# An attention-plus-GLU kernel: two raw weight buffers, an accumulating store and a reordered front

## The chip, the cores and the metric

The kernel runs on one core of one Trainium2 chip. The metric is the device time of one execution in microseconds (us); the time before is the median of 3 runs, 719.59 us (718.81 to 720.78). One more execution was profiled, and all rows of views are from it. The engines are called PE (TensorE, matrix products), DVE (VectorE), ACT (ScalarE), POOL (GpSimd) and SP (SyncE, which here only issues DMAs). Each engine works through its own instructions in order.

## The reference

The input x has 2048 tokens of width 448. It is layer-normalised without weights, and the output is x plus two branches on the normalised x: an attention with a memory, and a gated feed-forward layer. Cut to what matters:

```python
xn = _layernorm(x)
# attention: 16 heads of 28, 4 segments of 512 tokens
q, k, v = xn @ wq, xn @ wk, xn @ wv
for s in range(4):
    p = softmax(qs @ ks.T * scale + mask)      # mask: keys after the query
    o = g * (phi(qs) @ M) / (phi(qs) @ z + 1e-6) + (1 - g) * (p @ vs)
    M, z = M + phi(ks).T @ vs, z + phi(ks).sum()
# feed-forward: 448 -> 1792 -> 448
h = sigmoid(xn @ w_gate) * (xn @ w_up)
out = x + concat(o) @ wo + h @ w_down
```

## The kernel before, in words

**Precision.** Every operand of a large product is split in two parts: a rounded high part that ACT makes (`split`, L85-87, a copy) and the low rest that DVE makes (a subtraction). A product is then 11 matmuls: high by high, high by low, low by high (`TERMS`, L52). The width of 448 is held in four chunks of 128 rows, whose last holds high and low rows together, so matmuls of the fourth chunk need the low part as well.

**Front (L262-543).** For each of four blocks of 512 tokens: statistics, normalise, transpose on PE and split (`transpose_high`, `transpose_low`, L92-108), values (`value_terms`, L314), keys and queries (`keys_queries`, L330), which are stored in DRAM. For block 0 the order of the first three engines is written out by hand tile by tile (L387-483): `statistics`, `root` (a square root on ACT, L283), `rstd` and `normalise` (L288-309), `split_v` (a part of the value weights: high on ACT, low on POOL). From block 1 on, `recall` (L377) reads the memory: a matmul of `phi` with the state, `weigh` on DVE (L126), and a store of the result to `md` in DRAM from POOL's queue. It has two result buffers `tb` on the chip. The last block's four recalls stand between steps of the feed-forward generator, `FILL` = 3 steps ahead of each (L539-543).

**Feed-forward (`gated`, L158-256).** It is a generator, and PE's program is made by stepping it. The 14 slices of 128 hidden columns are taken in groups of two; a group passes the four blocks. Per block and slice: 22 gate-up matmuls `pgu` (L235), a tanh on ACT, two products on DVE, and later the down matmuls `pd` (L165), whose result DVE adds to `acc` (L168). The weights of a slice arrive as two loads on the SP queue: gate and up into `raw` (L173, one buffer) and down into `rawd` (L177, two buffers). `ready_up` and `ready_down` split them into `wgu` (three buffers, shared with others) and `wdn` (four). The table `ahead` (L212-226) says at which block and slot of a group each load and each split is called. The two halves of the output weights use `raw` as well (`load_out`, L191). One buffer means that a load can't be issued until ACT and DVE have split what is there.

**Attention (L551-708)** is a second generator, spread evenly over the feed-forward's steps by the loop at L750-759. 32 pairs of heads: query and key loads from DRAM (L563, two buffers `qk2`), score matmuls (L579) into two PSUM banks, a copy on ACT (L582), a mask on POOL (L591), maxima on DVE (L594), the shift by the maximum on DVE (L630), exp on ACT (L631). Two pairs make a unit: values by weights (`pa`, L656), a copy (L659), transposes (`n`, L663), `weigh`, and for segments 1 to 3 the memory's part, which is loaded from `md` into a tile `tb` (L648), is added by POOL (L668). The sum is stored to `od` from POOL's queue (L669). `project` (L710) later loads `od` block by block, transposes it, multiplies by wo and adds to `acc` (L742).

PE's order is the order in which the code is run. ACT, DVE, POOL and SP are ordered by a scheduler that the kernel's framework brings, outside the front's hand-written part. Tiles that share a buffer wait for each other by semaphores.

Of the kernel before, what the change touches and what calls it, by code (L numbers as in the profile page):

```python
# [9 lines left out]
F32 = mybir.dt.float32  # L10
F32R = mybir.dt.float32r
AF = mybir.ActivationFunctionType
ALU = mybir.AluOpType
# [3 lines left out]
P = 128  # L17
D = 448
# [36 lines left out]
FRONT = {mybir.EngineType.PE, mybir.EngineType.Activation, mybir.EngineType.DVE}  # L55
FILL = 3
WARM = 10
# [3 lines left out]
def kernel(  # L61
# [23 lines left out]
    def split(hi, lo, src):  # L85
        A.activation(hi, src, AF.Copy)  # L86
        V.tensor_sub(lo, src, hi.bitcast(F32))
# [52 lines left out]
    vd = [dram.tile([P, NT, H * 32], F32, name=f"vd{b}") for b in range(NB)]  # L140
    md = [dram.tile([P, NT, D], F32, name=f"md{b}") for b in range(NB)]
    od = [dram.tile([P, NT, D], F32, name=f"od{b}") for b in range(NB)]
# [15 lines left out]
    def gated():  # L158
# [14 lines left out]
        def load_up(f):  # L173
            raw_up[f] = mid.tile([P, 1024], F32, name="raw", bufs=1)
            nc.sync.dma_start(raw_up[f], w_ffn[f][:, :1024])

        def load_down(f):  # L177
            raw_down[f] = mid.tile([P, D], F32, name="rawd", bufs=2)
            nc.sync.dma_start(raw_down[f], w_ffn[f][:, 1024:])
# [8 lines left out]

        raw_o = {}

        def load_out(h):  # L191
            raw_o[h] = mid.tile([P, 1024], F32, name="raw", bufs=1)[:, :2 * D]
            nc.sync.dma_start(raw_o[h], w_o[:, 2 * D * h:2 * D * (h + 1)])

        def ready_out(h):
            wo[h] = eight_k(F32R, "wo").rearrange("p c n -> p (c n)")
            split(wo[h][:, :2 * D], wo[h][:, 2 * D:4 * D], raw_o[h])

# [5 lines left out]
        load_down(0)  # L204
        load_down(1)
        yield
# [3 lines left out]
        for f0 in range(0, NF, FG):  # L210

            ahead = {}  # L212
            if f0 == 0:
                ahead[0, 0] = lambda: ready_up(1)
            if f0 + FG < NF:
                ahead[0, 2] = lambda: load_up(f0 + 2)
                ahead[1, 2] = lambda: (ready_up(f0 + 2), load_down(f0 + 2))
                ahead[1, 3] = lambda: load_up(f0 + 3)
                ahead[2, 1] = lambda: (ready_down(f0 + 2), load_down(f0 + 3))
                ahead[3, 2] = lambda: ready_up(f0 + 3)  # L220
                ahead[3, 3] = lambda: ready_down(f0 + 3)
            else:

                ahead[0, 2] = lambda: load_out(0)
                ahead[1, 2] = lambda: (ready_out(0), load_out(1))
                ahead[3, 2] = lambda: ready_out(1)
# [35 lines left out]
    with tc.tile_pool(name="front", bufs=2) as sb, tc.manual_schedule(engines=FRONT):  # L262
# [24 lines left out]

        def rstd(mv, vh, y):  # L288

            steps = vh.shape[1]  # L290
            tm = sb.tile([P, steps], F32, name=f"tm{steps}")
            V.reciprocal(y, y)
            if steps == 1:
                V.tensor_scalar(tm, y, y, vh, op0=ALU.mult, op1=ALU.mult)
                V.tensor_scalar(y, tm, 1.5, y, op0=ALU.add, op1=ALU.mult)
            else:
                V.tensor_mul(tm, y, y)
                V.tensor_mul(tm, tm, vh)
                V.scalar_tensor_tensor(y, tm, 1.5, y, op0=ALU.add, op1=ALU.mult)
            return [(mv[:, t, 0:1], y[:, t:t + 1]) for t in range(steps)]  # L300

        def normalise(b, t, mean, y):
            xn = sb.tile([P, 512], F32, name="xn")
            V.tensor_scalar(xn[:, :D], acc[b][:, t, :], mean, y, op0=ALU.subtract, op1=ALU.mult)
            if b == 0:
                A.activation(xn[:, D:], xn[:, 384:D], AF.Copy)
            else:
                G.tensor_copy(xn[:, D:], xn[:, 384:D])
            return xn
# [67 lines left out]
        def recall(b, i, phi):  # L377
            tb = sb.tile([P, NT * HG, DH], F32, name="tb", bufs=2)
            n2 = bank("n2", ("m", "pd")[i % 2] if b < NB - 1 else "m")
            for t in range(NT):  # L380
                T.matmul(n2[:, t * P:(t + 1) * P], phi[:, t * P:(t + 1) * P], mst[b % 2][i], start=True, stop=True)  # L381
            weigh(sb, tb, n2, gate[:, HG * i:HG * (i + 1)], MEM_EPS)
            nc.gpsimd.dma_start(md[b][:, :, GW * i:GW * (i + 1)], tb.rearrange("p (t j) d -> p t (j d)", t=NT))

# [43 lines left out]

        def normalised(t):
            xn[t] = normalise(0, t, *rstd(*st[t], y[t])[0])  # L430

# [3 lines left out]
        normalised(0)  # L435
        split_v(0)
        st[1] = statistics(0, 1, 1)
        y[1] = root(st[1][1])
        split_v(1)
        turn_high(0)  # L440
# [19 lines left out]
        store_values(0, 1, pv[1])  # L460
        normalised(3)
        turn_low(2)
        pv = bank("pv", "p")
        value_terms(0, 2, pv, EARLY[1], 0, 5)
        turn_high(3)
        split_qk(0)
        value_terms(0, 2, pv, EARLY[1], 5)
        store_values(0, 2, pv)
# [11 lines left out]
        for b in range(NB):  # L480
# [57 lines left out]
            if last:  # L538
                phi = [phi_queries(b, i) for i in range(NG)]  # L539
                for i in range(NG):  # L540
                    for _ in range(FILL):
                        next(ffn)
                    recall(b, i, phi[i])
# [7 lines left out]
    class Pair:  # L551
# [53 lines left out]
        def weights(self, mx):  # L605
# [5 lines left out]
            V.tensor_max(m0[:, :, 8:16], m0[:, :, 8:16], mx[:, 64:80].rearrange("p (h n) -> p h n", h=2))  # L611
            up = sb.tile([P, 2, 16], F32, name="up", bufs=2)
            top = sb.tile([P, 2, 16], F32, name="top", bufs=2)
            G.tensor_copy(up[0:64], m0[64:128])
# [19 lines left out]
    class Unit:  # L634
# [9 lines left out]

        def load_memory(self):
            if self.s > 0:
                self.tb = sb.tile([P, NT, GW], F32, name="tb")
                nc.sync.dma_start(self.tb, md[self.s][:, :, GW * self.i:GW * (self.i + 1)])  # L648

        def finish(self):  # L650
# [15 lines left out]
            o3 = on.rearrange("p (t j) d -> p t (j d)", t=NT)  # L666
            if s > 0:
                G.tensor_add(o3, o3, self.tb)  # L668
            nc.gpsimd.dma_start(od[s][:, :, GW * i:GW * (i + 1)], o3)  # L669
            yield  # L670
# [4 lines left out]
    def attention():  # L675
# [5 lines left out]
        for u in range(len(units) + 1):  # L681
            for n in range(2):
                run[n] = pairs[2 * u + n].scores() if u < len(units) else iter(())
            for k, which in enumerate(SLOT):
# [15 lines left out]
                if which == 2 and u > 0:  # L700
                    fin = units[u - 1].finish()
                    next(fin)
                    units[u - 1].load_memory()
                    if u < len(units):
                        units[u].load_values()
# [44 lines left out]
    with tc.manual_schedule(engines=MANUAL):  # L750
        next(steps)
        k = NG * FILL + 6
        for part in (ffn, project()):
            for _ in part:
                want = min(round(n_att * (k - LEAD) / (N_FFN + N_OUT - LEAD - TAIL)), n_att)
                k += 1
                while done < want:
                    next(steps)
                    done += 1
# [38 lines left out]
```

## Time and profile before

| | |
|---|---|
| median of 3 runs | 719.59 us (718.81 to 720.78) |
| the profiled execution's own time | 719.77 us |
| its span in the trace | 718.0 us |
| PE busy | 703.8 us (98%) |
| DVE busy | 557.5 us (78%) |
| ACT busy | 338.2 us (47%) |
| POOL busy | 154.9 us (22%) |
| granted TensorE clock | 1.0 throughout |
| moved by DMA | 86.24 MB, mean 120 GB/s |

Times of a timeline row are the start in us from the span's start and the duration in us; behind the row stands in brackets how long the engine had been idle and what ended that (the releaser). In a list of waits each row gives who waited for whom, the sum, the number of times and the longest. A wait of PE costs time directly only if nothing else fills it, since PE runs its program in order. Idle time of the other engines costs nothing in itself.

### The profile page before, as it was taken

The numbers are of one execution on the slowest core, as the hardware profiler recorded it, in microseconds if no ns is written. First come the engines' busy times: TensorE is split into PE (matmuls) and PEld (weight loads), VectorE is DVE, ScalarE is ACT, GpSimd is POOL, SyncE is SP. The second block draws the span as 40 slices with busy tenths as digits, with TensorE's granted clock in tenths as the row PEclk, the third lists the DMA queues.
The fourth block names the chain that finished last, engine by engine and source line by source line (L and its number), as shares of the span: only waits on it lengthen the run. The fifth ranks groups of instructions, "written<-read, shape, count | busy, mean of one in ns | idle before, by whom it ended". The sixth has DMA issues, their size and how long they took to land.

```text
span 718.0 us, 10866 instructions
## 1 busy us (share of the span) xinstructions
PE 703.8 (98%) x3794; PEld 582.8 (81%) x3794; DVE 557.5 (78%) x1021; ACT 338.2 (47%) x557; POOL 154.9 (22%) x361
## 2 busy tenths in 40 slices
PE   7999999999999999999999999999999989999998
PEld 6898989887878787787877878778687777878797
DVE  6776685455888888888888998887898878889553
ACT  4745443232555565455555554545455453554120
POOL 3500010101222222222232422223132221231100
PEclk9999999999999999999999999999999999999999
DMA  8624546776233313421234323342332324222342
GB/s 306 254 118 177 201 187 228 254 248 177 65 97 104 91 43 97 119 77 54 70 107 119 90 60 117 82 115 66 83 94 79 79 70 113 64 74 86 98 148 90
DMA packets 52598, 86.24 MB, mean 120 GB/s; under 512 B 13888, under 2 KB 30464, under 8 KB 52032
## 3 DMA queue, kind: packets, MB, share of 16 engines
q1 hardware_dynamic: 50304, 79.13, 35.9%
q0 software_dynamic: 2240, 6.42, 2.7%
q8 instruction: 30, 0.49, 0.3%
q14 instruction: 24, 0.20, 0.1%
HBM read 53.81 MB, written 31.72 MB: 119 GB/s over the span
## 4 chain that ended last, share of the span: by engine, by line
PE 54%; DVE 23%; issue 11%; POOL 7%; ACT 3%; DMA 2%; POOLq 0%; SPq 0%; ACTq 0%
PE pgu L235 18%; PE pd L165 9%; PE pp L335 9%; DVE mx L594 6%; PE po L738 5%; PE pv L317 4%; DVE w L630 4%; DVE mb L622 3%; POOL w L591 3%; DVE acc L168 2%; PE st L579 2%; PE pa L656 2%; POOL on L668 2%; PE n L381 2%; PE pmm L363 1%
## 5 line engine op out<-in xcount | busy, mean ns | idle before, releaser
L235 PE MATMUL pgu<-xs,wgu 128*128 128x512 f32 x1232 | 321.7, 398 | 0.0
L235 PEld LDWEIGHTS pgu<-xs,wgu 128*128 128x128 f32 x1232 | 225.8, 188 | 44.8 <-issue 1.8
L165 PE MATMUL pd<-wdn,hh 128*128 128x448 f32 x672 | 164.2, 370 | 1.9 <-ACT wdn L86 1.0
L165 PEld LDWEIGHTS pd<-wdn,hh 128*128 128x128 f32 x672 | 122.3, 188 | 17.8 <-ACT wdn L86 1.4
L631 ACT ACTIVATE w<-w 128x1024 f32<-128x1024 f32 (+1 forms) x96 | 87.0, 915 | 91.4 <-DVE w L630 82.6
L591 POOL TENSOR_SCALAR_AFFINE_SELECT w<-w 128x256 f32<-128x256 f32 (+1 forms) x160 | 72.4, 457 | 234.9 <-ACT w L582 231.5
L594 DVE TRANSPOSE_TENSOR_REDUCE mx<-w 128x32 f32<-128x1024 f32 (+1 forms) x96 | 101.0, 1056 | 23.8 <-POOL w L591 23.7
L582 ACT ACTIVATE w<-st 128x512 f32<-128x512 f32 x160 | 93.1, 588 | 50.9 <-PE st L579 50.5
L630 DVE TENSOR_TENSOR w<-w,mb 128x1024 f32<-128x1024 f32 (+3 forms) x128 | 108.2, 868 | 0.4
L335 PE MATMUL pp<-xs,wqk 128*128 128x512 f32 x308 | 77.3, 399 | 0.0
L168 DVE TENSOR_TENSOR acc<-pd,acc 128x448 f32<-128x448 f32 x112 | 67.6, 605 | 4.1 <-PE pd L165 4.0
L579 PE MATMUL st<-qk 84*128 84x128 f32 (+3 forms) x256 | 64.2, 312 | 3.4 <-ACT w L582 3.4
L335 PEld LDWEIGHTS pp<-xs,wqk 128*128 128x128 f32 x308 | 56.6, 189 | 11.8
L246 ACT ACTIVATE hh<-sg 128x512 fp32r<-128x512 f32 x56 | 35.1, 627 | 54.5 <-DVE sg L244 51.6
L579 PEld LDWEIGHTS st<-qk 84*128 84x128 f32 x256 | 48.3, 189 | 13.6 <-ACT w L582 5.2
L622 DVE STREAM_TRANSPOSE mb<-top 128x1024 f32<-128x1024 f32 x32 | 39.8, 1243 | 15.2 <-POOL top L619 15.1
L243 ACT ACTIVATE sg<-pgu 128x512 f32<-128x512 f32 x56 | 33.1, 592 | 24.1 <-PE pgu L235 24.0
L247 DVE SCALAR_TENSOR_TENSOR hh<-sg,hh 128x512 fp32r<-128x512 f32 x56 | 39.7, 709 | 4.6 <-ACT hh L246 4.4
L341 DVE TENSOR_TENSOR qk<-pp,qk 128x512 fp32r<-128x512 f32 x28 | 19.4, 691 | 30.5 <-ACT e L340 23.6
L336 ACT ACTIVATE qk<-pp 128x512 fp32r<-128x512 f32 x28 | 16.7, 597 | 50.3 <-PE pp L335 34.2
L244 DVE SCALAR_TENSOR_TENSOR sg<-sg,pgu 128x512 f32<-128x512 f32 x56 | 37.3, 666 | 3.9 <-PE pgu L235 3.8
L317 PE MATMUL pv<-wv,xs 128*128 128x448 f32 x176 | 39.1, 373 | 0.8 <-DVE xs L108 0.8
(98 smaller groups left out, 647.3 us busy)
## 6 DMA issues: line engine op xcount, KB each, us to landing
qk<-qd SPq DMA_DIRECT2D x192, 112.0 KB
qd<-qk SPq DMA_DIRECT2D x28, 512.0 KB
raw<-in_w_ffn SPq DMA_DIRECT2D x14, 512.0 KB
vd<-vst SPq DMA_DIRECT2D x4, 1024.0 KB
vv<-vd SPq DMA_DIRECT2D x16, 256.0 KB
od<-on POOLq DMA_DIRECT2D x16, 224.0 KB, 3.8
ob<-od SPq DMA_DIRECT2D x4, 896.0 KB
out<-acc SPq DMA_DIRECT2D x16, 224.0 KB
```

Source lines behind the costliest of these rows:

```text
L165: T.matmul(pd[:, :D], l, r, start=n == 0, stop=n == len(mms) - 1)
L168: V.tensor_add(acc[b][:, t, :], pd[:, :D], acc[b][:, t, :])
L235: T.matmul(dst, wgu[f][:, w, side * P:(side + 1) * P], xs[b][:, a, :], start=n == 0, stop=n == len(TERMS) - 1)
L317: T.matmul(pv[:, :D], xs[b][:, a, t * P:(t + 1) * P], wv[:, w, :], start=n == 0, stop=n == len(TERMS) - 1)
L335: T.matmul(pp, wqk[c][:, w, :], xs[b][:, a, :], start=n == 0, stop=n == len(TERMS) - 1)
L579: T.matmul(st[:, at:at + L - kb * P], self.qk[:KS, 1, h, kb * P:(kb + 1) * P], self.qk[:KS, 0, h, kb * P:], start=True, stop=True)
L582: A.activation(w, st, AF.Copy)
L591: G.affine_select(d, d, pattern=pattern, base=0, channel_multiplier=-1, compare_op=ALU.is_ge, fill=MASK)
L594: V.tensor_reduce(mx[:, 16 * n0:16 * (n + 1)], self.w[:, n0 * L:(n + 1) * L].rearrange("p (b n) -> p b n", n=32), axis=mybir.AxisListType. ...
L622: V.transpose(mb.rearrange("p h (b n) -> p (h b) n", n=32), top.rearrange("p h b -> p (h b)").unsqueeze(2).to_broadcast([P, 32, 32]))
L630: V.tensor_sub(w[:, :, a:b], w[:, :, a:b], mb[:, :, q0:])
L631: A.activation(w, w, AF.Exp, scale=SCALE)
```

## The change

1. **Raw buffers.** `raw` gets two buffers, `rawd` one. The table `ahead` is rewritten: gate-up loads are called earlier, down loads later, each after the split that frees the one buffer. The down weights of slice 1 are loaded into a `raw` buffer, and those of slice 2 are loaded inside the first group, behind the first query loads. The output weights' two halves become the 15th and 16th gate-up load.
2. **Accumulating store.** `recall` stores to `od` itself; `md` is gone. A unit's store of segments 1 to 3 adds to what is there (`accum_op=ALU.add`). POOL's add, the load and the tile `tb` of the unit are gone.
3. **Fills.** The last block's recalls have 4, 3, 2 and 1 steps ahead of them in place of 3 each, and all blocks' recalls alternate between two banks.
4. **Front of block 0.** Statistics and root of the second tile come before the first split of the value weights. The fourth tile is normalised by POOL (three instructions and a copy that were DVE's and ACT's). Ten in place of five value matmuls of the third tile stand ahead of the fourth tile's transposes.
5. `up` and `top`, two small tiles of the maxima, get one buffer each.

```diff
-FILL = 3
+FILLS = (4, 3, 2, 1)
...
         def load_up(f):
-            raw_up[f] = mid.tile([P, 1024], F32, name="raw", bufs=1)
-            nc.sync.dma_start(raw_up[f], w_ffn[f][:, :1024])
+            raw_up[f] = mid.tile([P, 1024], F32, name="raw", bufs=2)
+            if f < NF:
+                nc.sync.dma_start(raw_up[f], w_ffn[f][:, :1024])
+            else:
+                nc.sync.dma_start(raw_up[f][:, :2 * D], w_o[:, 2 * D * (f - NF):2 * D * (f - NF + 1)])
...
+        def load_down(f, tag="rawd"):
+            raw_down[f] = (mid.tile([P, 1024], F32, name="raw", bufs=2)[:, :D] if tag == "raw" else
+                           mid.tile([P, D], F32, name="rawd", bufs=1))
...
             if f0 == 0:
-                ahead[0, 0] = lambda: ready_up(1)
+                ahead[0, 0] = lambda: (load_down(1, "raw"), ready_up(1))
+                ahead[0, 2] = lambda: load_up(2)
+                ahead[1, 3] = lambda: (load_down(2), load_up(3))
             if f0 + FG < NF:
-                ahead[0, 2] = lambda: load_up(f0 + 2)
-                ahead[1, 2] = lambda: (ready_up(f0 + 2), load_down(f0 + 2))
-                ahead[1, 3] = lambda: load_up(f0 + 3)
+                ahead[1, 2] = lambda: ready_up(f0 + 2)
                 ahead[2, 1] = lambda: (ready_down(f0 + 2), load_down(f0 + 3))
+                ahead[2, 2] = lambda: load_up(f0 + 4)
                 ahead[3, 2] = lambda: ready_up(f0 + 3)
                 ahead[3, 3] = lambda: ready_down(f0 + 3)
+                if f0 > 0:
+                    ahead[0, 2] = lambda: (load_up(f0 + 3), load_down(f0 + 2))
             else:
-                ahead[0, 2] = lambda: load_out(0)
-                ahead[1, 2] = lambda: (ready_out(0), load_out(1))
+                ahead[0, 2] = lambda: load_up(f0 + 3)
+                ahead[1, 2] = lambda: ready_out(0)
                 ahead[3, 2] = lambda: ready_out(1)
...
-            n2 = bank("n2", ("m", "pd")[i % 2] if b < NB - 1 else "m")
+            n2 = bank("n2", ("m", "pd")[i % 2])
...
-            nc.gpsimd.dma_start(md[b][:, :, GW * i:GW * (i + 1)], tb.rearrange("p (t j) d -> p t (j d)", t=NT))
+            nc.gpsimd.dma_start(od[b][:, :, GW * i:GW * (i + 1)], tb.rearrange("p (t j) d -> p t (j d)", t=NT))
...
         normalised(0)
-        split_v(0)
         st[1] = statistics(0, 1, 1)
         y[1] = root(st[1][1])
+        split_v(0)
         split_v(1)
...
-        normalised(3)
+        normalised(3, G)
         turn_low(2)
         pv = bank("pv", "p")
-        value_terms(0, 2, pv, EARLY[1], 0, 5)
+        value_terms(0, 2, pv, EARLY[1], 0, 10)
         turn_high(3)
         split_qk(0)
-        value_terms(0, 2, pv, EARLY[1], 5)
+        value_terms(0, 2, pv, EARLY[1], 10)
...
-                    for _ in range(FILL):
+                    for _ in range(FILLS[i]):
                         next(ffn)
                     recall(b, i, phi[i])
...
-            if s > 0:
-                G.tensor_add(o3, o3, self.tb)
-            nc.gpsimd.dma_start(od[s][:, :, GW * i:GW * (i + 1)], o3)
+            nc.gpsimd.dma_start(od[s][:, :, GW * i:GW * (i + 1)], o3, accum_op=ALU.add if s > 0 else ALU.bypass)
```

What the change moves on ACT is shown at the place where slice 12's gate-up weights are split, `wgu` from `raw` (L86), in the sixth of seven groups. The other rows are the tanh (`sg`), the high part of the product (`hh`), score copies (`w` from `st`), exponentials (`w` from `w`) and the copy of values by weights (`w` from `pa`). Before:

```order
L243 ACTIVATE sg_5283<-pgu_5227 128x512
L631 ACTIVATE w_5068<-w_5068 128x2x512 x2
L582 ACTIVATE w_5192<-st_5268 128x512
L582 ACTIVATE w_5192<-st_5289 128x512
L631 ACTIVATE w_5068<-w_5068 128x512
L246 ACTIVATE hh_5286<-sg_5283 128x512
L86 ACTIVATE wgu_5686<-raw_5465 128x1024
L659 ACTIVATE w_5068<-pa_5331 128x512
```

Now, in the lines of the changed kernel:

```order
L244 ACTIVATE sg_5263<-pgu_5207 128x512
L632 ACTIVATE w_5046<-w_5046 128x2x512 x2
L583 ACTIVATE w_5172<-st_5248 128x512
L86 ACTIVATE wgu_5662<-raw_5073 128x1024
L632 ACTIVATE w_5046<-w_5046 128x512
L583 ACTIVATE w_5172<-st_5269 128x512
L247 ACTIVATE hh_5266<-sg_5263 128x512
L655 ACTIVATE w_5046<-pa_5311 128x512
```

The split has moved ahead of the pair's last exponential, of one score copy and of `hh`.

On PE the order differs in two places. In the front (value matmuls `pv`, transposes `pt`, the first key-query matmuls `pp`) before:

```order
L100 MATMUL pt<-ident,xn 128x128 x4
L317 MATMUL pv<-wv,xs_67 128x448 x18
L100 MATMUL pt<-ident,xn 128x128 x4
L317 MATMUL pv<-wv,xs_67 128x448 x9
L100 MATMUL pt<-ident,xn 128x128 x4
L317 MATMUL pv<-wv,xs_67 128x448 x17
L335 MATMUL pp<-xs_67,wqk_112 128x512 x11
```

Now:

```order
L100 MATMUL pt<-ident,xn 128x128 x4
L318 MATMUL pv<-wv,xs_67 128x448 x18
L100 MATMUL pt<-ident,xn 128x128 x4
L318 MATMUL pv<-wv,xs_67 128x448 x14
L100 MATMUL pt<-ident,xn 128x128 x4
L318 MATMUL pv<-wv,xs_67 128x448 x12
L336 MATMUL pp<-xs_67,wqk_108 128x512 x11
```

Five value matmuls of the third tile have passed from behind to ahead of the fourth tile's transposes. The second place is the last four recalls (`n`, by memory state `mst_0` to `mst_3`) between gate-up matmuls, up to the first scores (`st`). Before:

```order
L235 MATMUL pgu<-xs_67,wgu 128x512 x14
L381 MATMUL n_1576<-mst_0_123,phi 128x128 x4
L235 MATMUL pgu<-xs_67,wgu 128x512 x11
L381 MATMUL n_1608<-mst_1_124,phi 128x128 x4
L235 MATMUL pgu<-xs_68,wgu 128x512 x12
L381 MATMUL n_1632<-mst_2_125,phi 128x128 x4
L235 MATMUL pgu<-xs_68,wgu 128x512 x11
L381 MATMUL n_1662<-mst_3_126,phi 128x128 x4
L235 MATMUL pgu<-xs_68,wgu 128x512 x10
L579 MATMUL st<-qk_1689 128x512
```

Now:

```order
L236 MATMUL pgu<-xs_67,wgu 128x512 x18
L382 MATMUL n_1579<-mst_0_119,phi 128x128 x4
L236 MATMUL pgu<-xs_67,wgu 128x512 x7
L236 MATMUL pgu<-xs_68,wgu 128x512 x4
L382 MATMUL n_1609<-mst_1_120,phi 128x128 x4
L236 MATMUL pgu<-xs_68,wgu 128x512 x7
L382 MATMUL n_1628<-mst_2_121,phi 128x128 x4
L236 MATMUL pgu<-xs_68,wgu 128x512 x4
L382 MATMUL n_1645<-mst_3_122,phi 128x128 x4
L236 MATMUL pgu<-xs_68,wgu 128x512 x18
L580 MATMUL st<-qk_1672 128x512
```

The sum ahead of the first scores is 58 either way; the first recall is four matmuls later, the last one eight earlier. Behind the first scores PE's order is the same as before.

More of the change, by code (lines that the diff above doesn't have):

```diff
@@ L140 @@
     vd = [dram.tile([P, NT, H * 32], F32, name=f"vd{b}") for b in range(NB)]
-    md = [dram.tile([P, NT, D], F32, name=f"md{b}") for b in range(NB)]
     od = [dram.tile([P, NT, D], F32, name=f"od{b}") for b in range(NB)]
@@ L173, in load_up @@
         def load_up(f):
-            raw_up[f] = mid.tile([P, 1024], F32, name="raw", bufs=1)
-            nc.sync.dma_start(raw_up[f], w_ffn[f][:, :1024])
-        def load_down(f):
-            raw_down[f] = mid.tile([P, D], F32, name="rawd", bufs=2)
+            raw_up[f] = mid.tile([P, 1024], F32, name="raw", bufs=2)
[6 more added lines that the diff above has]
+                           mid.tile([P, D], F32, name="rawd", bufs=1))
             nc.sync.dma_start(raw_down[f], w_ffn[f][:, 1024:])
@@ L187, in ready_down @@
             split(wdn[f][:, 0, :], wdn[f][:, 1, :], raw_down[f])
[L189 to L193, printed above, removed]
         def ready_out(h):
             wo[h] = eight_k(F32R, "wo").rearrange("p c n -> p (c n)")
-            split(wo[h][:, :2 * D], wo[h][:, 2 * D:4 * D], raw_o[h])
+            split(wo[h][:, :2 * D], wo[h][:, 2 * D:4 * D], raw_up[NF + h][:, :2 * D])
         begin.append(lambda: (ready_down(0), ready_down(1)))
@@ L204, in gated @@
         load_down(0)
-        load_down(1)
         yield
@@ L286, in root, with rstd @@
             return y
-        def rstd(mv, vh, y):
+        def rstd(mv, vh, y, eng=V):
             steps = vh.shape[1]
@@ L293, in rstd @@
             if steps == 1:
-                V.tensor_scalar(tm, y, y, vh, op0=ALU.mult, op1=ALU.mult)
-                V.tensor_scalar(y, tm, 1.5, y, op0=ALU.add, op1=ALU.mult)
+                eng.tensor_scalar(tm, y, y, vh, op0=ALU.mult, op1=ALU.mult)
+                eng.tensor_scalar(y, tm, 1.5, y, op0=ALU.add, op1=ALU.mult)
             else:
@@ L300, in rstd, with normalise @@
             return [(mv[:, t, 0:1], y[:, t:t + 1]) for t in range(steps)]
-        def normalise(b, t, mean, y):
+        def normalise(b, t, mean, y, eng=V):
             xn = sb.tile([P, 512], F32, name="xn")
-            V.tensor_scalar(xn[:, :D], acc[b][:, t, :], mean, y, op0=ALU.subtract, op1=ALU.mult)
-            if b == 0:
+            eng.tensor_scalar(xn[:, :D], acc[b][:, t, :], mean, y, op0=ALU.subtract, op1=ALU.mult)
+            if b == 0 and eng is V:
                 A.activation(xn[:, D:], xn[:, 384:D], AF.Copy)
@@ L427, in turn_low, with normalised @@
             transpose_low(p3[t], xs[0], t)
-        def normalised(t):
-            xn[t] = normalise(0, t, *rstd(*st[t], y[t])[0])
+        def normalised(t, eng=V):
+            xn[t] = normalise(0, t, *rstd(*st[t], y[t], eng)[0], eng)
         p3, xn, st, y = {}, {}, {}, {}
@@ L611, in weights @@
             V.tensor_max(m0[:, :, 8:16], m0[:, :, 8:16], mx[:, 64:80].rearrange("p (h n) -> p h n", h=2))
-            up = sb.tile([P, 2, 16], F32, name="up", bufs=2)
-            top = sb.tile([P, 2, 16], F32, name="top", bufs=2)
+            up = sb.tile([P, 2, 16], F32, name="up")
+            top = sb.tile([P, 2, 16], F32, name="top")
             G.tensor_copy(up[0:64], m0[64:128])
@@ L643, in load_values @@
             nc.sync.dma_start(self.vv, vd[self.s][:, :, self.i * P:(self.i + 1) * P])
[L645 to L648, printed above, removed]
         def finish(self):
@@ L702, in attention @@
                     next(fin)
-                    units[u - 1].load_memory()
                     if u < len(units):
@@ L751 @@
         next(steps)
-        k = NG * FILL + 6
+        k = sum(FILLS) + 6
         for part in (ffn, project()):
```

## The prediction

> **What bounds the kernel now.** I read the busy times first, then what TensorE (PE) waited for, then the timeline around each of those waits. The first rows are the head of the page, one group of its part 5 (last columns: busy us, mean ns of one, idle before) and one piece of the chain that ended last (start, us, what).
>
> ```profile
> span 718.0 us, 10866 instructions
> PE 703.8 (98%) x3794; PEld 582.8 (81%) x3794; DVE 557.5 (78%) x1021; ACT 338.2 (47%) x557; POOL 154.9 (22%) x361
> L235 PEld LDWEIGHTS pgu<-xs,wgu 128*128 128x128 f32 x1232 | 225.8, 188 | 44.8 <-issue 1.8 <-DVE e L345 0.2
> 646.00 2.56 PE pgu L235 x11
> ```
>
> PE is busy for 703.8 of 718.0 us, so 14.2 us of idle time are all that this view shows to win. Eleven gate-up matmuls take 2.56 us, 233 ns each, and each loads its weights for 188 ns. [...] So an idle stretch that goes from PE's row should go from the time, and nothing else will. The change takes no matmul away.
>
> These are all PE waits over 0.3 us but the one at the very start (waits by engine: us in total, times, longest), then two rows of the same view for ScalarE (ACT).
>
> ```profile
> PE st L579 <- ACT w L582: 3.4, 4, 1.5
> PE n L663 <- ACT w L659: 1.6, 1, 1.6
> ...
> PE pt L100 <- DVE xn L304: 1.2, 1, 1.2
> PE pd L165 <- ACT wdn L86: 1.0, 1, 1.0
> PE pv L317 <- DVE xs L108: 0.8, 1, 0.8
> PE pd L165 <- DVE acc L742: 0.7, 1, 0.7
> ```
>
> ```profile
> ACT wgu L86 <- DMA raw<-in_w_ffn: 6.1, 3, 4.0
> ...
> ACT wo L86 <- DMA raw<-in_w_o: 3.1, 1, 3.1
> ```
>
> ACT stood 9.2 us for weights that were still being loaded. The timeline shows where PE paid for it (start, us, engine line; in brackets the idle time before and what ended it).
>
> ```profile
> 435.38 1.06 ACT L86 ACTIVATE wgu<-raw 128x1024 fp32r<-128x1024 f32 x1 [3.95 <-DMA raw<-in_w_ffn]
> ...
> 437.50 0.50 PE L579 MATMUL st<-qk 84*128 84x512 f32 x1 [0.52 <-ACT w L582]
> ```
>
> ```profile
> 508.75 0.36 SPq L175 DMA_DIRECT2D raw<-in_w_ffn  x1
> 513.67 1.06 ACT L86 ACTIVATE wgu<-raw 128x1024 fp32r<-128x1024 f32 x1 [1.61 <-DMA raw<-in_w_ffn]
> ...
> 515.27 0.33 PE L663 MATMUL n<-ident,w 128*128 128x128 f32 x1 [1.57 <-ACT w L659]
> ...
> 590.75 0.50 PE L579 MATMUL st<-qk 84*128 84x512 f32 x1 [1.55 <-ACT w L582]
> ...
> 644.27 0.50 PE L579 MATMUL st<-qk 84*128 84x512 f32 x1 [1.04 <-ACT w L582]
> ```
>
> One raw buffer means that a load is issued only when the split before it is done: at 508.75 for a split that then starts at 513.67. Behind that split, in order on ACT, stand the copies that free PE's banks or feed it. So 0.52, 1.57 and, behind the first half of the output weights, 1.55 us of PE are due to the single buffer.
>
> **Two raw buffers.** The three waits sum to 3.64 us, and I count all of it. In the new order a gate-up load is called more than half a group of two slices before its split (the splits at 435.38 and 513.67 are one group apart: 78 us). What is late next: the splits still wait until PE has left the weight buffer that they write. Those at 435 and 588 had ACT idle for 3.95 and 3.1 us in front of them while PE lost 0.52 and 1.55, so they may stay late by over a microsecond and still cost nothing. At 513 the split moves three ACT instructions ahead, and the copy at L659 then has only a normal copy before it.
>
> Splits that move ahead on ACT now stand in front of other score copies. The four score waits sum to 3.4 us, and 0.52, 1.55 and 1.04 of it are quoted, so the fourth was 0.29; it stood behind a split whose data was long there. With three splits moved, the cost lies between nothing and 0.9 us; I take 0.1, for nine such splits cost 0.29 together.
>
> **One down buffer, and the third down load behind the queries.** On the SP queue each down load now waits for the split of the one before, and the query loads behind it wait too. This is the SP queue's own wait for such splits now.
>
> ```profile
> SPq L179 <- DVE wdn L87: 23.1, 7, 12.7
> ```
>
> The queue has stood there for up to 12.7 us, and no row of PE's waits names a query load: they are made two pairs ahead. Cost nothing; the cover is that lead, and each microsecond beyond it would be one of PE.
>
> **Attention's part added by the store.** This removes twelve GpSimd (POOL) adds, twelve loads on the SP queue and the wait of the store for the add. Rows of the groups, then of the DMA issues (last: us to landing), then of the timeline:
>
> ```profile
> L668 POOL TENSOR_TENSOR on<-on,tb 128x448 f32<-128x448 f32 x12 | 16.1, 1344 | 42.7 <-DVE on L136 42.5
> L669 POOL DMA_DIRECT2D od<-on x16 | 11.6, 724 | 14.1 <-DVE on L136 11.0 <-POOL on L668 2.9
> ```
>
> ```profile
> od<-on POOLq DMA_DIRECT2D x16, 224.0 KB, 3.8
> ```
>
> ```profile
> 427.39 1.15 POOL L668 TENSOR_TENSOR on<-on,tb 128x448 f32<-128x448 f32 x1 [5.14 <-DVE on L136]
> ...
> 427.76 1.33 DVE L630 TENSOR_TENSOR w<-w,mb 128x512 f32<-128x512 f32 x1
> ```
>
> ```profile
> 508.60 0.68 DVE L630 TENSOR_TENSOR w<-w,mb 128x512 f32<-128x512 f32 x1
> ```
>
> POOL is busy for 22% of the span, so its 16.1 us are worth nothing in themselves. Beside an add, VectorE's (DVE) subtraction took 1.33 us in place of 0.68; that returns up to 0.65 x 12 = 7.8 us of DVE, which PE doesn't wait for directly: no value in the sum. An accumulating store is not in this trace. Bounds: its issue as now (724 ns) or dearer. Up to 1344 + 724 = 2068 ns POOL is no later than today. I take the near row, 724. Its landing may take three times 3.8 us: the output projection reads a block's rows long after, so nothing waits.
>
> **The front.** These are ACT's first split and the root behind it, then PE to the first key-query matmul.
>
> ```profile
> 7.02 0.58 ACT L407 ACTIVATE wv<-wv_raw 128x448 fp32r<-128x448 f32 x1 [0.67 <-DMA wv_raw<-in_w_v]
> 7.50 0.19 ACT L285 ACTIVATE y<-vh 128x1 f32<-128x1 f32 x1
> ```
>
> ```profile
> 9.11 0.33 PE L100 MATMUL pt<-ident,xn 128*128 128x128 f32 x1 [1.23 <-DVE xn L304]
> ```
>
> ```profile
> 16.67 0.68 PE L317 MATMUL pv<-wv,xs 128*128 128x448 f32 x2 [0.84 <-DVE xs L108]
> ...
> 17.18 0.60 PE L100 MATMUL pt<-ident,xn 128*128 128x128 f32 x4
> ```
>
> ```profile
> 17.54 3.73 PE L317 MATMUL pv<-wv,xs 128*128 128x448 f32 x17
> ...
> 19.03 0.29 DVE L108 TENSOR_TENSOR xs<-pt,xs 64x128 fp32r<-64x128 f32 x1
> ...
> 21.10 0.39 PE L335 MATMUL pp<-xs,wqk 128*128 128x512 f32 x1
> ```
>
> The second tile's root no longer stands behind the first split, which waited for its DMA: 7.50 becomes about 7.04, and the wait at 9.11 shrinks by 0.46. The wait at 16.67 goes, since DVE no longer normalises the fourth tile before it lowers the third. But five matmuls move ahead of the fourth tile's transposes. From these (17.18) to the end of its low part (19.32) are 2.14 us. Before, 0.36 of transposes and nine matmuls of 219 ns came in between, 2.33: no wait. Now 0.36 and four, 1.24: a new wait of 0.90 for the old 0.84. Sum of the front: -0.46 + 0.06 = -0.40; at best -1.3, if the new wait doesn't come.
>
> The normalising itself is off DVE; on POOL it must end before PE reaches those transposes. Its cost there is not in the trace: at most a two-input add (1344) and three short ones, of which this is the nearest:
>
> ```profile
> L308 POOL COPY xn<-xn 128x64 f32<-128x64 f32 x12 | 3.1, 261 | 37.0 <-DVE xn L304 36.9
> ```
>
> 1344 + 3 x 261 = 2.1 us; beside it run the third tile's transposes, copy and low part (2.14 by the fourth's) and seven matmuls: hidden. If it is slower, I allow +0.5.
>
> **Recalls, fills.** As many gate-up matmuls as before stand ahead of the first scores; the last recall comes eight earlier, with eight more behind it. The wait for the first down split stays: its place on ACT, behind the same gate, doesn't change.
>
> ```profile
> 170.59 1.03 ACT L86 ACTIVATE wdn<-rawd 128x448 fp32r<-128x448 f32 x2
> ...
> 171.21 0.47 PE L165 MATMUL pd<-wdn,hh 128*128 128x448 f32 x1 [0.97 <-ACT wdn L86]
> ```
>
> New: second and fourth recall are 12 matmuls closer, 2.8 us, and use the same two store buffers. A store held its buffer from 159.62 to 165.29:
>
> ```profile
> 159.62 0.71 POOL L383 DMA_DIRECT2D md<-tb  x1 [22.35 <-DVE tb L136]
> ```
>
> ```profile
> 165.29 0.62 DVE L136 TENSOR_TENSOR tb<-n,rc 128x448 f32<-128x448 f32 x1 [0.35 <-DMA md<-tb]
> ```
>
> DVE may stand up to 2.8 us for it, and eight more matmuls (1.9) cover most: 0 to +0.9, I take +0.2.
>
> **Sum.** The profiled execution took 719.77, 1.77 beside its span. -3.64 + 0.1 - 0.40 + 0.2 = -3.7: 716.1. The three runs' median is 719.59, 0.18 less: **715.9**.
>
> **Rivals.** *More is won.* The scores' other waits, 0.29 and 1.04 (at 644.27), follow DVE's subtractions, and these lose the adds beside them: 715.9 - 1.33 = 714.6. For it: 1.33 against 0.68. Against: no add runs just before 644.27. [...] Chance 0.15.
>
> *The gain is given back.* DVE, not ACT, is what attention follows in its second half:
>
> ```profile
> 520.00:540.00 20.00, 20.00 (x96) 17.18 (x95) 18.94 (x32) 11.40 (x18) 6.93 (x13) 1.00 0.30 89
> ```
>
> 18.94 of 20 us are DVE's here (third pair). PE's waits at 515 and 590 let DVE catch up; without them PE meets it later, and 1.57 + 1.55 return as longer score waits: 719.0. Against: DVE is 78% busy over the span. 0.21.
>
> *The loads come no earlier*, since the SP queue holds them behind query loads that wait for PE: the front alone is left, 719.2. Against: half a group of lead. 0.04.
>
> *Slower.* The accumulating store takes POOL longer than 2068 ns to issue; past that, masks (L591) queue behind it, and maxima, weights and PE after them. At 3 us: 12 x 0.93 = 11.2 more, 727.1. For it: the form isn't in the trace. Against: a plain store takes 724 ns. 0.07.
>
> **How the numbers follow.** Forecast 0.53. This kernel's measurement tells about 0.3%, 2.2 us, from no change: faster is below 717.4. That is the forecast, more won and a small part of given back: 0.70; same 0.23, slower 0.07. The low end is 715.9 less 1.33, the front's 0.9 and some: 713.2. The high end takes in the given-back case: 719.3.
>
> **What would show it.** After: ACT's waits for raw loads gone, and no PE waits of 0.5, 1.6 and 1.5 us at 435, 513 and 588; the first key-query matmul at 20.7; a PE wait behind the fourth transposes; 0.97 still there before the first down matmul; the store's issue near 0.72. I am wrong if these waits go and the waits for score copies grow by as much, or if POOL's issue row exceeds 2 us.

## The result, and the profile after

The changed kernel takes 714.17 us (median of 6 executions, 713.73 to 715.95) against 720.16 us of the kernel before on the same chips: ratio 0.9921, 95% interval 0.9906 to 0.9935. The profiled execution took 713.91 us, with a span of 712.2. The forecast was 715.9, so faster by about two more. Within the 5.9 us between the two profiled executions the terms of the sum were off in both directions.

The head of the page, then the list of PE's waits in the changed kernel, whole (us in total, times, longest):

```profile
span 712.2 us, 10816 instructions
PE 702.3 (99%) x3794; PEld 582.4 (82%) x3794; DVE 551.3 (77%) x1018; ACT 338.9 (48%) x556; POOL 146.2 (21%) x353
```

```profile
PE warm L419 <- POOL ident masks.py:199: 1.6, 1, 1.6
PE pt L100 <- DVE xn L305: 1.4, 2, 0.7
PE pd L164 <- ACT wdn L86: 1.0, 1, 1.0
PE pd L164 <- DVE acc L735: 0.7, 1, 0.7
PE pv L318 <- ACT xs L102: 0.5, 1, 0.5
PE pt L100 <- ACT xn L307: 0.4, 1, 0.4
PE pk L356 <- DVE e L346: 0.3, 1, 0.3
PE pd L164 <- DVE wdn L87: 0.2, 1, 0.2
```

No row for scores (`st`) or for the transposes at the end of a unit (`n`) is left: the 3.4 and the 1.6 us of before are gone whole, with the waits at 581 and 644 that the sum had left standing. ACT's list now has 0.3 us for `raw`, where 9.2 stood, and 1.7 for the single `rawd`, which cost PE nothing. In the timeline these are the five matmuls that had waited, and then, on ACT, the two weight splits that stood ahead of the first two:

```profile
437.34 0.40 PE L580 MATMUL st<-qk 84*128 84x512 f32 x1
...
513.26 0.60 PE L659 MATMUL n<-ident,w 128*128 128x128 f32 x4
...
578.71 0.40 PE L580 MATMUL st<-qk 84*128 84x512 f32 x1
...
586.46 0.40 PE L580 MATMUL st<-qk 84*128 84x512 f32 x1
...
638.27 0.40 PE L580 MATMUL st<-qk 84*128 84x512 f32 x1
```

```profile
433.92 1.06 ACT L86 ACTIVATE wgu<-raw 128x1024 fp32r<-128x1024 f32 x1 [1.93 <-PE pgu L236]
...
507.13 1.05 ACT L86 ACTIVATE wgu<-raw 128x1024 fp32r<-128x1024 f32 x1
```

The first of these splits now waits 1.93 us for PE to leave the weight buffer, not for a load, and costs PE nothing, as the prediction said. The second shows no wait. Against before the five matmuls start 0.16, 2.01, 2.52, 4.29 and 6.00 us earlier (437.34 against 437.50, and so on). The first key-query matmul starts later, at 21.92 against 21.10. So the front lost 0.82, and from there to the fifth place 6.82 us were won, with 4.97 us of idle time at these places in PE's row.

The front, on PE and ACT:

```profile
9.62 0.33 PE L100 MATMUL pt<-ident,xn 128*128 128x128 f32 x1 [0.43 <-ACT xn L307]
...
19.29 2.79 PE L318 MATMUL pv<-wv,xs 128*128 128x448 f32 x11 [0.48 <-ACT xs L102]
21.92 2.26 PE L336 MATMUL pp<-xs,wqk 128*128 128x512 f32 x9
```

```profile
7.08 0.20 ACT L286 ACTIVATE y<-vh 128x1 f32<-128x1 f32 x1 [0.68 <-DVE vh L281]
7.89 1.04 ACT L408 ACTIVATE wv<-wv_raw 128x448 fp32r<-128x448 f32 x2 [0.61 <-DMA wv_raw<-in_w_v]
9.32 0.24 ACT L307 ACTIVATE xn<-xn 128x64 f32<-128x64 f32 x1
```

The root came at 7.08, close to the forecast 7.04. A new wait of the value terms is there, but it is 0.48 us, not 0.90, and it is for ACT's high part, not for DVE's low one. But the second tile's copy (9.32) now stands behind both splits, whose weights landed at 7.89 instead of 7.02.

POOL's groups, and the store's landing:

```profile
L663 POOL DMA_DIRECT2D od<-on x16 | 17.6, 1098 | 51.4 <-DVE on L136 51.4
...
L305 POOL TENSOR_SCALAR xn<-acc,mv,y 128x448 f32<-128x448 f32 x1 | 1.9, 1876 | 0.1
```

```profile
od<-on POOLq DMA_DIRECT2D x16, 224.0 KB, 4.4
```

The store's issue is 1098 ns in the mean, not 724 (about 1.22 us where it accumulates), still under the 2068 from which POOL would be later than before. The normalising took 1876 ns against an allowance of 1344 for this one instruction.

### The profile page after: what moved, and what is told of

It is laid out like the page before. It is cut to its first block, busy times and chain, and to the rows that moved or that the text cites. A ratio compares the mean times of both kernels' runs of the same rounds, so it can differ in the third digit from the quotient of the medians.

```text
span 712.2 us, 10816 instructions
## 1 busy us (share of the span) xinstructions
PE 702.3 (99%) x3794; PEld 582.4 (82%) x3794; DVE 551.3 (77%) x1018; ACT 338.9 (48%) x556; POOL 146.2 (21%) x353
## 3 DMA queue, kind: packets, MB, share of 16 engines
q0 software_dynamic: 7616, 6.42, 5.9%
## 4 chain that ended last, share of the span: by engine, by line
PE 90%; issue 4%; DVE 2%; DMA 2%; ACT 1%; POOL 0%; SPq 0%; POOLq 0%; DVEq 0%
PE pgu L236 38%; PE pd L164 20%; PE pp L336 6%; PE st L580 5%; PE po L731 5%; PE pa L652 5%; PE pv L318 5%; PE pmm L364 1%; PE n L659 1%; PE pt L100 1%; PE n L382 1%; DMA wv_raw<-in_w_v 1%; PE pk L356 1%; PE pt L98 1%; DMA od<-tb 1%
## 5 line engine op out<-in xcount | busy, mean ns | idle before, releaser
L631 DVE TENSOR_TENSOR w<-w,mb 128x1024 f32<-128x1024 f32 (+3 forms) x128 | 102.8, 827 | 0.5
```

What stands on the lines that cost most here:

```text
L631: V.tensor_sub(w[:, :, a:b], w[:, :, a:b], mb[:, :, q0:])
```

## The experiments

In the timed executions the granted clock is listed too, and it matters below: a value of 0.996 to 0.998 (a low clock below) in place of 0.999 or 1.000 (full clock) goes with some 2 us in several of these kernels.

**The changed kernel again.** No edit.

> The changed kernel once more, unchanged, beside the front experiments. In its first profile the raw weights of the values landed 0.87 us later than in the kernel before (first split at 7.89 us against 7.02), and the first key-query matmul started at 21.92 us against 21.10. Theory A (the late landing was chance of that execution, as the loads are issued in the same order in both kernels): the first split starts anywhere between 7.0 and 7.9, and the first key-query matmul follows it, 21.4 to 21.9. Theory B (the new order makes it late): 7.9 and 21.9 again. Both expect 714.2 us within 1.5.

Measured 715.44 us (713.41 to 715.54; ratio 0.9938, 0.9924 to 0.9951). Theory A for the front: the first split starts at 7.09 here and the key-query matmuls at 21.47, so at least half of the 0.82 was chance. Not expected: five of six executions had a clock of 0.997 or 0.998 and took 715.28 to 715.54; the one at 1.000 took 713.41. The profile shows where. First DVE and PE, then the busy times of a stretch of both executions, this one first (us; PE, PEld, DVE, ACT, POOL busy; clock; DMA share; GB/s):

```profile
169.10 0.62 DVE L136 TENSOR_TENSOR tb<-n,rc 128x448 f32<-128x448 f32 x1 [2.36 <-DMA od<-tb]
```

```profile
171.98 0.47 PE L164 MATMUL pd<-wdn,hh 128*128 128x448 f32 x1 [1.54 <-ACT wdn L86]
```

```profile
172.00:178.00 6.00, 5.81 (x19) 4.65 (x20) 2.99 (x4) 1.58 (x4) 0.73 (x2) 0.72 0.39 128
```

```profile
172.00:178.00 6.00, 5.81 (x27) 4.82 (x28) 3.60 (x5) 2.32 (x5) 1.02 (x3) 1.00 0.39 127
```

The second recall's store still held its buffer when the last recall came, DVE stood 2.36 us, the gate-up products and the down split behind it came late, and PE waited 1.54 us. Then the clock fell to one half for about 3.4 us: 19 matmuls in six microseconds instead of 27. In the first profile of this kernel the wait was 1.00 and the clock stayed.

**The front in parts.** With the old front:

```diff
+        split_v(0)
         st[1] = statistics(0, 1, 1)
         y[1] = root(st[1][1])
-        split_v(0)
...
-        normalised(3, G)
+        normalised(3)
...
-        value_terms(0, 2, pv, EARLY[1], 0, 10)
+        value_terms(0, 2, pv, EARLY[1], 0, 5)
...
```

> The changed kernel with the old front: split before the second tile's root, the fourth tile normalised by VectorE, five value matmuls ahead of its transposes. Theory A (GpSimd's 1.88 us normalising and the five moved matmuls cost 0.3 us, the late weights were chance): first key-query matmul at 21.1 to 21.5, 713.5 to 713.9 us. Theory B (the whole 0.82 us by which the front is later is the change's): 21.1 and 713.4. My prediction's front (a gain of 0.40) would make it 714.6 and put that matmul 0.4 later than in the changed kernel.

Measured 713.71 us (713.15 to 715.54); the four executions at full clock took 713.15 to 713.76. With only the last two edits (root still first):

> The changed kernel with the second tile's root still ahead of the first split, but the fourth tile normalised by VectorE and five value matmuls ahead of its transposes. If GpSimd and the five matmuls are what costs the front, and the order of the root gains up to 0.46 where the weights land as before: first key-query matmul 20.6 to 21.1, 713.0 to 713.5 us. If the order of the root is what makes the front late: 21.6 and 714.0, like the changed kernel.

Measured 715.21 us, four of six at a low clock; the two others 713.30 and 713.61. Key-query at 21.23 behind a split at 7.27. With the first and the last edit (GpSimd still normalises):

> The changed kernel with the old order of split and root and five value matmuls, but the fourth tile still normalised by GpSimd. GpSimd's normalised tile was ready at 17.9 us in the changed kernel, when fourteen value matmuls had run; with five fewer, PE reaches the fourth tile's transposes 1.1 us earlier and must wait that much longer for the same tile, but has the five matmuls left to cover the lowering behind. If GpSimd is the cost: a wait of 1.0 to 1.4 us before the fourth tile's transposes and the first key-query matmul at 21.5 to 21.9, 714.0 to 714.4 us. If the order of the root is the cost and GpSimd's time is covered: 21.1 and 713.4.

Measured 714.48 us, three of six at a low clock, the others 713.43 to 713.89. The wait for GpSimd came, as the first reading said it would, at 0.92 us in place of 1.0 to 1.4:

```profile
17.24 0.66 PE L100 MATMUL pt<-ident,xn 128*128 128x128 f32 x4 [0.92 <-POOL xn L305]
```

The medians of these four can't rank the fronts, since the clock moves them by more. The distance from ACT's first split to the first key-query matmul can. With the old front it is 14.07 to 14.09 us in six profiles (this experiment, the kernel before and four below), whenever the weights landed: the splits started between 6.55 and 7.87. With the new front it is 14.38 to 14.42 in three profiles whose splits started at 7.09 to 7.34, and 14.03 or 14.04 in three with 7.64 to 7.97. With only the root ahead it is 13.96, with only POOL's normalising 14.41. So the new front loses 0.3 us when the weights come early and gains 0.05 when they come late. It may lose more when they come earlier still: at 7.09 the split stood right behind the root (6.98) and no longer waited for the weights, and with the old order of the root three splits started as early as 6.55, 6.77 and 6.80.

Two stretches of this distance tell the edits apart. From the first split to the third tile's transposes it is 6.55 to 6.57 us with the old order of the root, in seven profiles; with the root ahead it is 6.17 or 6.18 where the weights came late, 6.54 or 6.55 where they came early, and 6.44 with only the root ahead. From there to the first key-query matmul it is 7.51 to 7.53 wherever DVE normalises the fourth tile and 7.84 to 7.87 wherever POOL does. So the order of the root gains between nothing and 0.38 us, and POOL's normalising costs 0.33 each time.

Where the root's gain is lost, POOL's half of the split started close to DVE's normalising of the second tile: 0.25 and 0.05 us before it in two profiles, 0.06 behind its start in the third. In the changed kernel's second profile POOL started at 7.73, and the normalising took

```profile
7.98 1.14 DVE L305 TENSOR_SCALAR xn<-acc,mv,y 128x448 f32<-128x448 f32 x1
```

and in its first profile, where it began at 8.07 and POOL at 8.55, 0.51 us. With only the root ahead it began at 7.81, 0.12 us before POOL at 7.93, and took 0.51 us too.

**The add back, without the load.** `G.tensor_add(o3, o3, o3)` ahead of the accumulating store in the changed kernel.

> The changed kernel with a GpSimd add put back where the old one stood (blocks 1 to 3: the unit's output is added to itself, so attention's part of these blocks is doubled), without the load and with the accumulating store. Theory D (the score waits of 0.29 us at 581 and 1.04 at 644, 0.45 and 1.21 from start to start, went because the adds went): both come back and the sum is 1.2 to 1.7 us more than the changed kernel's 713.4 to 714.4 at full clock, 715.0 to 716.0; VectorE's subtractions go from 827 ns back to about 868. Theory E (they went because two raw buffers moved the splits on ScalarE): no such wait, 713.4 to 714.4.

Measured 715.02 us (714.10 to 716.26; two of five at a low clock, the others 714.10 to 715.02). DVE's subtractions went from 827 to 851 ns, but no score wait came back. Theory E: the waits at 581 and 644 did not go with the adds.

**The store alone.** The kernel before with `accum_op` in the store; `md`, the add and the load are gone.

> The kernel before with the accumulating store alone: no add, no load back, one raw gate-up buffer, the old front and fills. Theory D: PE's waits at 581 and 644 are gone, those at 435, 513 and 588 stay, 719.2 less 1.66, 717.5 us. Theory E: all five stay, 719.2. The part of my prediction that gave the store no value also says 719.2.

Measured 717.19 us (716.25 to 717.38), ratio 0.9968 (0.9955 to 0.9980): the size that theory D gave, but not at its places. These are PE's score waits:

```profile
PE st L578 <- ACT w L581: 1.6, 4, 0.5
```

They are 0.30 at 550, where none was before, 0.55 at 580, 0.24 at 589 and 0.48 at 642. So the stalls at 435, 513 and 588 are gone or nearly so, though there is one raw buffer, and those at 581 and 644 are not. The rows at 580 show how an add reached a weight load. Before: POOL, then DVE, ACT (the split and, further on, that of the output weights) and the SP queue.

```profile
580.40 1.14 POOL L668 TENSOR_TENSOR on<-on,tb 128x448 f32<-128x448 f32 x1 [4.87 <-DVE on L136]
```

```profile
580.18 0.61 DVE L168 TENSOR_TENSOR acc<-pd,acc 128x448 f32<-128x448 f32 x1
580.73 1.36 DVE L247 SCALAR_TENSOR_TENSOR hh<-sg,hh 128x512 fp32r<-128x512 f32 x1
...
583.05 1.30 DVE L87 TENSOR_TENSOR wgu<-raw,wgu 128x1024 fp32r<-128x1024 f32 x1
```

```profile
579.13 1.04 ACT L86 ACTIVATE wgu<-raw 128x1024 fp32r<-128x1024 f32 x1
...
588.74 0.95 ACT L86 ACTIVATE wo<-raw 128x896 fp32r<-128x896 f32 x1 [3.09 <-DMA raw<-in_w_o]
```

```profile
584.41 6.79 SPq L193 DMA_DIRECT2D raw<-in_w_o  x2
```

With the store alone:

```profile
579.96 0.69 DVE L246 SCALAR_TENSOR_TENSOR hh<-sg,hh 128x512 fp32r<-128x512 f32 x1
...
581.50 1.31 DVE L87 TENSOR_TENSOR wgu<-raw,wgu 128x1024 fp32r<-128x1024 f32 x1
```

```profile
578.36 1.04 ACT L86 ACTIVATE wgu<-raw 128x1024 fp32r<-128x1024 f32 x1
...
586.66 0.95 ACT L86 ACTIVATE wo<-raw 128x896 fp32r<-128x896 f32 x1 [2.54 <-DMA raw<-in_w_o]
```

```profile
582.88 6.25 SPq L192 DMA_DIRECT2D raw<-in_w_o  x2
```

Beside the add a DVE product took 1.36 instead of 0.69 us. DVE's half of the split stands behind it, and the one raw buffer is free only after that half. From ACT's half (579.13 and 578.36) to DVE's half it was 3.92 us and is now 3.14; the load goes out as much earlier. From its issue to its split it took 0.55 us less besides (3.78 in place of 4.33), for which no cause is shown. So PE's wait at 590.75 fell from 1.55 to 0.24.

**Which of the two: the add or the load.** First the store alone with the self-add, no load:

> The accumulating store alone (717.2 us) with a GpSimd add put back ahead of it (the output of blocks 1 to 3 added to itself, so doubled), but no load on the SP queue. One raw buffer. If the store alone gained by the add that is gone (VectorE's half of a weight split and its subtractions run beside it and are slower, so the one raw buffer comes free later): back to 718.7 to 719.4, with the waits at 515 and 588 near 1.6 again. If it gained by the load that is gone from the SP queue: 717.2 stays, within 0.4.

Measured 720.07 us (719.10 to 721.74), ratio 1.0010 (1.0001 to 1.0019): the whole gain of the store is gone, and more than the 718.7 to 719.4 expected. Five of eleven executions had a low clock; the median of the others is 719.79. Three of the waits of before are back: 0.90 at 438, 1.23 at 515, and the one behind the output weights, where the clock falls after it:

```profile
591.10 0.50 PE L578 MATMUL st<-qk 84*128 84x512 f32 x1 [2.14 <-ACT w L581]
```

```profile
592.00:596.00 4.00, 4.00 (x14) 3.33 (x13) 3.49 (x9) 1.11 (x3) 1.09 (x5) 0.57 0.83 245
```

At this last place ACT's and DVE's halves were 3.70 us apart, against 3.14 with the store alone, and the load took 5.02 us from issue to split, against 3.78. So the larger part of this one stall is the load's own time; whether the add has to do with that is open.

Then a load of 8 columns where the old one stood, with an add of these columns alone:

> The accumulating store alone (717.2 us) with a load put back on the SP queue where the old one stood (8 columns of each row tile, waiting for its one buffer as the old one did) and a GpSimd add of only these columns, about 0.3 us in place of 1.34; blocks 1 to 3 have these columns changed. One raw buffer. If the add was what cost: 717.2, within 0.4. If the load was: 718.7 to 719.4.

Measured 715.93 us (715.39 to 716.39), ratio 0.9950 (0.9937 to 0.9962). The full add was the cost, not the load's place in the queue. That it is 1.3 us below the store alone neither theory expected. Of the 1.45 us between the two profiles 0.57 is in the front, where the weights landed at 7.30 instead of 7.87 and the first key-query matmul started at 21.37 instead of 21.94; the rest is open.

**Two raw buffers with the add and the load.** Both put back into the changed kernel: the small load, and a full add that reads it.

> The changed kernel with both the old add and the old load put back as traffic: a small load (8 columns of each row tile) on the SP queue where the old load stood, and a full-size GpSimd add that reads it ahead of each accumulating store, so the output of blocks 1 to 3 has that added to it. With two raw buffers. If two raw buffers by themselves remove the five stalls of before (theory E): no score wait over 0.3 us, at full clock 713.4 to 714.6. If they need the add or the load gone (theory D, or the queue: a load on the SP queue that waits for an add holds the weight loads behind it): two or more stalls back, 715.0 to 717.0 at full clock.

Measured 714.40 us (713.82 to 715.37), ratio 0.9930 (0.9917 to 0.9942). No score wait is back, with DVE's subtractions at 851 ns. Theory E: the two buffers with their new table are enough for all five places, without what the store saves. From the first down matmul to the end it is 540.28 us here, 540.31 in the changed kernel, 543.62 with the store alone and 546.84 before. No run has the two buffers in the kernel before and nothing else.

**Even fills.** `FILLS = (3, 3, 3, 3)` and the last block's recalls on one bank.

> The changed kernel with three gate-up matmul groups ahead of each recall and the last block's recalls on one bank, as before. In the runs of the changed kernel and of the front experiments so far the times fall in two groups, 713.2 to 714.4 at a clock of 0.999 or 1.000 (16 of 30) and 714.9 to 716.0 at 0.996 to 0.998 (14 of 30); in two profiles of the second group the clock falls for some 6 us right behind the first down matmul, which had waited 1.36 and 1.54 us for its weights, after VectorE had stood 2.2 and 2.4 us for a recall's store buffer. Theory C (the closer recalls make that wait longer, and the long wait lets the clock fall): here the wait is about 1.0, VectorE's 0.4, and at most one run in six is at the low clock: median 713.4 to 714.2. Rival (the dip is chance and has nothing to do with the fills): three of six low, median 713.4 to 715.5.

Measured 713.78 us (713.52 to 713.86), all four at 0.999 or 1.000. DVE waits 0.81 before the third recall and 0.23 before the last, PE 0.98 for the first down split.

**A third recall buffer**, with the old front and then with the new one: `name="tb", bufs=3`.

> The changed kernel with the old front (split first, VectorE normalises, five) and a third buffer for the recalls' stores, so that no recall waits for a store. Theory C: VectorE no longer stands 1.7 to 2.4 us before the last recall, the gate-up products behind it and ScalarE's first down split come earlier by up to that, the first down matmul waits 0 to 0.5 us in place of 1.45, the clock doesn't fall: 712.0 to 712.8 us. Rival (the split is held by something else): the wait stays over 1 us, 713.2 to 715.5 as with the old front alone.

Measured 712.94 us (712.60 to 713.59), ratio 0.9912 (0.9898 to 0.9925). All four executions at 0.999 or 1.000. DVE's wait is gone. PE's is not, so the shorter wait that theory C expected did not come, nor its 712.0 to 712.8 us: the split now stands behind a tanh of ACT that waits 1.20 us for its gate-up matmuls.

```profile
170.59 0.47 PE L164 MATMUL pd<-wdn,hh 128*128 128x448 f32 x1 [0.98 <-ACT wdn L86]
```

> The changed kernel with its own front and a third buffer for the recalls' stores, nothing else. Theory C (the wait for a recall's store lets the clock fall): no run at a clock under 0.999, VectorE's wait before the last recall gone, the first down matmul waits about 1.0 us, and the front costs 0.3 us beside the same kernel with the old front (712.94): 713.0 to 713.6. Rival (chance): about half of the runs at 0.996 to 0.998 and 714.9 to 715.6.

Measured 713.49 us (713.32 to 713.64), ratio 0.9916 (0.9902 to 0.9929), all five at 0.999 or 1.000. That is 0.55 us above the same with the old front, but on another chip, and the intervals of the two ratios overlap; the distance above gives 0.33.

Theory C fits: with the 4, 3, 2, 1 fills and two buffers 18 of 40 executions of six kernels had a clock of 0.998 or less; with even fills or a third buffer none of 13. But 14 of the 18 are from the 24 executions on one chip, on which neither even fills nor a third buffer were timed. In the sessions that have both kinds it is 3 of 10 against none of 13, so a difference between chips is not ruled out. The version with the old front and the third buffer has the lowest median of all.

## Why the prediction was right or wrong

**Two raw buffers: right, and too small.** The loads come early enough, what is late next costs nothing, and the two buffers do it without the store's help. Two steps of the sum failed. "So an idle stretch that goes from PE's row should go from the time" took the idle column for the price: from the matmul at 437 to that at 515 the kernel won 1.85 us for an idle time of 1.57, and from that at 581 to that at 590 1.77 for 1.55. That is 0.2 to 0.3 us a stall that the row counts as busy. And 0.29 and 1.04 were left out as not due to the buffer; with the add and the load put back they stayed away, so the buffers remove them too. Together it is 6.8 us from the front on, instead of 3.6. Of this the two profiles lost 0.82 in the front, where the first split started 0.87 later because the weights landed later; with either front that start varies by 0.9 us or more from profile to profile, so this part is chance.

**Splits that move ahead, 0.1:** no score wait is left, so nothing.

**More is won** had nearly the right time for the wrong reason: those two waits went, but not because of the adds beside DVE's subtractions.

**Attention's part added by the store, no value.** True in this change only because the raw buffers come with it: with them, add and load back cost at most some tenths. Alone it is worth 2.2 us (717.19 against 719.36). The step that failed is "DVE, which PE doesn't wait for directly": at the place shown the one raw buffer was freed by DVE's half of the split, behind a product that the add made slow. The slower issue, 1.22 us, hurt nobody, as the bound of 2068 said.

What ran beside POOL shows in two places. At 580 the product of two SBUF tiles took 1.36 us beside the add, against 0.69 with the store alone, and the sum that reads `pd` from PSUM, 0.39 of it beside the same add, took 0.61, within the 0.56 to 0.63 of all 112 such sums. In the front, with the root ahead, the normalising, which has one tile as input, took 1.14 to 1.44 us in the three profiles where POOL's half of the split started before it or 0.06 us behind its start, and 0.51 in the four where POOL started 0.12 us or more behind its start.

**The front: wrong sign.** -0.40 was forecast; 14.38 to 14.42 us in place of 14.08 make it +0.3, or nothing when the weights are late. Both terms failed. "The wait at 9.11 shrinks by 0.46" came to 0.38 with late weights and to nothing with early ones. It left out that DVE's normalising may then run beside POOL's half of the split: 1.14, 1.32 and 1.44 us in three profiles instead of 0.51. And +0.06 for the fourth tile was +0.33 in every profile with POOL's normalising. Of the four value matmuls counted ahead of the new wait only one ran; the others are the fourth tile's own and need ACT's high part of it, which came 1.29 us after its transposes began. POOL's normalising also held PE's weight load for 0.3 us, within the 0.5 allowed. The medians can't price the front: on the one chip known to have timed both, the changed kernel's only execution at full clock took 713.41 us, and the old front's four took 713.15 to 713.76.

**Recalls and fills, +0.2: the place was right, the price was not.** DVE stood 1.7 to 2.4 us before the last recall, within the 2.8 given, and in four of seven profiles 0.2 to 1.2 us before the third as well. The cover by eight matmuls was counted for DVE, but behind DVE stands the chain to the first down split. From the first key-query matmul to the first down matmul it is 149.94 and 149.96 us with the third buffer, 150.10 before, and 149.99 to 150.75 in the seven profiles with two buffers and the new fills: from -0.1 to +0.65 against before. The clock's fall was in no term. A low clock came in nearly half of these executions. In the changed kernel's second profile, which has the fall, the rest from the first down matmul on took 541.86 us, against 540.31 in its first: 1.55 more, beside a wait that was 0.54 longer.

**Not seen:** DVE giving the gain back, loads held by the SP queue, a store over 2068 ns.

## What to carry to other kernels

A single buffer filled through a chain of engines is freed by the last of them, so anything that slows that engine, even one that is off the critical path, decides when the next load goes out (here some 0.8 us later at 584, behind one DVE product of 1.36 us instead of 0.69); a second buffer cuts the whole chain at once (here all five waits, 4.97 us in PE's row). Price a stall from start to start of the same matmuls in two traces, not by the idle column. And look what stands behind a wait of a microsecond or two on TensorE: here a wait that was 0.5 us longer came with a fall of the clock that cost 1.55 us.

## What the runs showed of the hardware

The clock fell to one half behind PE waits of 1.54 us and 2.14 us, quoted above, and of 1.36 us with GpSimd's normalising and the old order of the root. Read from windows of 1 us, the three falls lasted 3.40, 3.42 and 3.42 us in this order, not some 6 as the expectation for the even fills has it. The third wait:

```profile
171.57 0.47 PE L164 MATMUL pd<-wdn,hh 128*128 128x448 f32 x1 [1.36 <-ACT wdn L86]
```

The clock didn't fall behind the 1.57 us of before, nor behind a longer one in the changed kernel with the add and the load put back, whose profiled clock was 1.0:

```profile
172.75 0.47 PE L164 MATMUL pd<-wdn,hh 128*128 128x448 f32 x1 [1.74 <-ACT wdn L86]
```

So the length of the wait alone does not tell the falls from the rest: 1.36 us had one, 1.57 and 1.74 us had none. What decides was not shown.

The accumulating store of 224 KB made the software queue's packets rise from 2240 to 7616 in all, 528 instead of 80 for each of the twelve, at the same 6.42 MB; its issue took about 1.22 us instead of 0.72, and the median landing of the sixteen stores was 4.4 instead of 3.8.
